# A weight's low word scaled and multiplied in one VectorE instruction, and two buffers for each conversion instead of three

## The chip, the cores and the metric

The kernel runs on one core of a Trainium2 chip. The metric is device time in microseconds; the kernel before took a median of 1023.06 us over 3 runs (1022.12 to 1026.41).

## What is computed

An attention layer feeds a mixing layer. Only the shapes and the arithmetic matter here; the weights `w_ch1` and `w_ch2` are 64-bit floats, all else is 32-bit.

```python
# attention: batch 4, 8 heads, 1152 keys, head size 64; queries pooled in pairs to 576
q_pool = q.reshape(B, H, S // 2, 2, D).mean(axis=3)
scores = np.matmul(q_pool, k.transpose(0, 1, 3, 2)) / np.sqrt(D)
attn = softmax(scores)                       # max subtracted, 1e-9 added to the sum
x = np.matmul(attn, v)                       # -> (B, 576, 512)
# mixing: real part of a 2-D FFT, layer norm, a feed-forward pair 512 -> 2048 -> 512
X = np.fft.fft(np.fft.fft(x, axis=1), axis=2)
u = x + np.real(X)
un = (u - u.mean(-1)) / np.sqrt(var(u) + 1e-6)
ch = np.maximum(un @ w_ch1, 0.0) @ w_ch2
return u + ch
```

## The kernel before

Attention runs over 16 pairs of heads, five units of 128 query columns to a pair. A unit has score matmuls (L220) whose negated, running-minimum copy VectorE takes out of PSUM (L222), an exponential on ScalarE (L234), transposes (L247) that ScalarE or VectorE copies out as `pt` (L250), and the product with `v` (L263, `o`). The queries and keys of the next heads are made meanwhile: GpSimd adds the two halves of `qr` (L186) and forms the low part of `ks` (L189), ScalarE casts `qh` (L194), GpSimd forms `ql` (L197).

Behind each batch of attention come its Fourier matmuls (`dft`: L501, L509), its norm (`norm`: L541 to L600) and its feed-forward (`ffn`): 32 blocks of weights for a batch, `w1` and `w2` in turns of four. A block is 12 matmuls of 128x512 at L689 to L691 (three products of high and low parts, four times). A block of `w1` ends in a ReLU on ScalarE (L708) and its low part `g` on VectorE (L709). These are fills between attention units.

The weights come as 64-bit floats. `convert` turns each of the 32 blocks into a high and a low 32-bit part once, while attention runs, and stores the result in DRAM, from where `wload` (L681) loads it for each batch. One conversion reads `wraw` from DRAM (L620, three buffers), takes the absolute value of the high word on ScalarE (L629), clamps, shifts, merges the sign and masks it on VectorE (L631, L633, L639, L642), scales the low word on ScalarE (`rest`, L635), casts the high part on ScalarE (L646), and then does three operations on GpSimd in two halves each (L649): `rest` times the power of two in `wa`, `wb` minus the high part, and the sum of the two. L655 stores it. `wa`, `rest` and `wb` are three tiles out of one ring of four (tag `cv`).

The order of all this is not left to a scheduler. The program keeps a clock of its own, `now`, which advances by what each step of attention yields; `after(wait, fn)` puts a step at a later point of that clock, and `convert` is a generator whose yields are such waits. So each engine's queue is a fixed list in order, and a yield that is changed moves instructions in it. `inside` lets one conversion at a time between its first ScalarE step and its last GpSimd step. `going` is non-empty once the first feed-forward has begun.

The ring `x` has five buffers for attention's results, each of which holds half a batch; where a sixth is wanted, `drain` stops attention and emits feed-forward blocks alone, each as soon as the plan has the conversion of the block two ahead in `wsc`. The first drain stands at about 430 to 470 us of the trace, beside the norm of batch 1; the last conversions are emitted within it. SyncE's queue issues nearly all DMAs, in order: raw weights (L620), stores (L655), loads (L681), and the heads' inputs (L126, L127).

## Time and profile before

| what | us |
|---|---|
| median of 3 runs | 1023.06 |
| the profiled execution | 1021.06 |
| its span, first to last instruction | 1019.3 |
| TensorE matmul busy | 968.8 |
| VectorE busy | 602.5 |
| ScalarE busy | 529.1 |
| GpSimd busy | 396.0 |

TensorE's busy time is modelled and overlaps from one matmul to the next, so a busy stretch isn't one at its peak. The conversions run from 80 us to 477 us; in that part of the span VectorE, ScalarE and GpSimd have most of their work. The profiled execution lies 2.0 us under the median.

### The profile page before, as it was taken

Reading aid. Unit: us, or ns where it says so; the run is one execution under the profiler, and the core shown is the slowest. Engines: PE = TensorE matmul, PEld = TensorE weight load, DVE = VectorE, ACT = ScalarE, POOL = GpSimd, SP = SyncE. Lnnn points to the kernel's source line nnn. Section 1 sums busy time; section 2 is a strip of 40 time slices with the busy share of each in tenths; the row PEclk is TensorE's granted clock in tenths of the full one; section 3 lists DMA queues with packets and bytes.
Section 4 is the critical chain, followed back from the end, with each engine's and each line's share of the span. In section 5 each row is a group of like instructions: output and inputs, shape, how many; then the busy total and the mean of one; then the engine's idle time right before and its main releaser. Section 6 shows DMA issues by size and latency. Waiting matters only on the chain.

```text
span 1019.3 us, 19742 instructions
## 1 busy us (share of the span) xinstructions
PE 968.8 (95%) x7392; PEld 841.5 (83%) x7392; DVE 602.5 (59%) x1526; ACT 529.1 (52%) x1033; POOL 396.0 (39%) x577
## 2 busy tenths in 40 slices
PE   6999988999999999978999999999999999899998
PEld 5898877777788887867888888788888878799998
DVE  5557787888756798866544465745644274422222
ACT  5777877758755575565644454535744221301100
POOL 3555678766666786874523232222400000000000
PEclk9999999999899999999999999999999999999999
DMA  6645458645385877566565453345432445733434
GB/s 181 176 142 183 130 189 255 191 139 167 119 255 208 280 242 235 182 235 197 175 194 164 135 184 120 90 150 161 130 116 83 145 137 165 219 131 128 128 124 124
DMA packets 62515, 170.91 MB, mean 168 GB/s; under 512 B 16770, under 2 KB 20242, under 8 KB 62420
## 3 DMA queue, kind: packets, MB, share of 16 engines
q1 hardware_dynamic: 58100, 151.96, 47.4%
q0 software_dynamic: 4320, 17.70, 5.5%
q8 instruction: 58, 0.95, 0.4%
q14 instruction: 37, 0.30, 0.1%
HBM read 146.88 MB, written 22.75 MB: 166 GB/s over the span
## 4 chain that ended last, share of the span: by engine, by line
PE 51%; DVE 3%; DMA 2%; ACT 1%; issue 1%; POOL 1%; SPq 0%; DVEq 0%; ACTq 0%
PE f L689 7%; PE f L691 6%; PE f L690 6%; PE o L263 6%; PE s L220 6%; PE t L247 5%; PE t L689 5%; PE t L691 5%; PE t L690 5%; DMA w<-w 1%; DVE sp L222 1%; DMA qr<-in_q 1%; PE f L509 1%; PE t L509 1%; ACT pt L250 0%
## 5 line engine op out<-in xcount | busy, mean ns | idle before, releaser
L222 DVE TENSOR_SCALAR_CACHE_REDUCE sp<-s,bia 128x384 f32<-128x384 f32 x288 | 177.5, 616 | 89.6 <-PE s L220 67.5
L220 PE MATMUL s<-ks,qh 128*128 128x384 f32 x480 | 185.1, 386 | 17.3 <-ACT qh L164 6.3
L234 ACT ACTIVATE sp<-sp,bia 128x1152 f32<-128x1152 f32 x144 | 180.2, 1255 | 5.7 <-DVE sp L222 5.4
L250 ACT COPY pt<-t 128x512 f32<-128x512 f32 (+2 forms) x243 | 124.7, 527 | 98.7 <-PE t L247 95.5
L263 PE MATMUL o<-pt,vs 128*64 128x128 f32 (+1 forms) x2880 | 168.1, 271 | 1.1 <-DVE pt L250 0.9
L263 PEld LDWEIGHTS o<-pt,vs 128*64 128x64 f32 x2880 | 148.9, 140 | 23.4 <-issue 20.1
L220 PE MATMUL s<-ks,ql 128*128 128x384 f32 x480 | 164.1, 342 | 0.9 <-POOL ql L197 0.9
L247 PE MATMUL t<-ident,sp 128*128 128x128 f32 x1045 | 151.7, 277 | 3.0 <-DVE sp L222 2.0
L247 PEld LDWEIGHTS t<-ident,sp 128*128 128x128 f32 x1045 | 121.0, 141 | 25.5 <-issue 7.0
L189 POOL TENSOR_TENSOR ks<-kr,ks 64x288 fp32r<-64x288 f32 x120 | 101.9, 880 | 37.3 <-issue 15.9
L220 PEld LDWEIGHTS s<-ks,qh 128*128 128x128 f32 x480 | 92.2, 192 | 28.1 <-ACT pt L250 10.1
L220 PEld LDWEIGHTS s<-ks,ql 128*128 128x128 f32 x480 | 92.6, 193 | 2.1 <-POOL ql L197 1.2
L709 DVE SCALAR_TENSOR_TENSOR g<-f,g 128x512 fp32r<-128x512 f32 (+1 forms) x49 | 32.5, 663 | 99.4 <-ACT g L708 99.4
L708 ACT ACTIVATE g<-f 128x512 fp32r<-128x512 f32 (+1 forms) x49 | 28.2, 576 | 120.0 <-PE f L691 120.0
L222 DVE TENSOR_SCALAR_CACHE_REDUCE sp<-s 128x384 f32<-128x384 f32 x144 | 78.7, 547 | 9.6 <-PE s L220 8.3
L197 POOL TENSOR_TENSOR ql<-qr,qh 128x288 fp32r<-128x288 f32 (+2 forms) x75 | 54.2, 747 | 75.6 <-ACT qh L194 74.6
L689 PE MATMUL f<-unh,w 128*128 128x512 f32 (+1 forms) x196 | 77.4, 395 | 6.3 <-DMA w<-w 5.8
L649 POOL TENSOR_TENSOR rest<-rest,wa 128x256 f32<-128x256 f32 x64 | 48.8, 781 | 88.9 <-DVE wa L642 69.9
L186 POOL TENSOR_TENSOR qr<-qr 128x288 f32<-128x288 f32 x60 | 48.1, 820 | 78.5 <-DMA qr<-in_q 78.5
L689 PE MATMUL f<-g,w 128*128 128x512 f32 (+1 forms) x192 | 76.0, 396 | 2.3 <-DMA w<-w 1.1
L691 PE MATMUL f<-unl,w 128*128 128x512 f32 (+1 forms) x196 | 75.1, 383 | 0.0
L690 PE MATMUL f<-unh,w 128*128 128x512 f32 (+1 forms) x196 | 74.8, 381 | 0.0
(146 smaller groups left out, 1749.8 us busy)
## 6 DMA issues: line engine op xcount, KB each, us to landing
w<-w SPq DMA_DIRECT2D x128, 512.0 KB, 3.6
qr<-in_q SPq DMA_DIRECT2D x30, 576.0 KB, 4.3
ks<-in_k POOLq DMA_DIRECT2D x30, 576.0 KB, 6.2
wraw<-in_w SPq DMA_DIRECT2D x32, 512.0 KB, 3.9
w<-wraw SPq DMA_DIRECT2D x32, 512.0 KB, 3.0
vs<-in_v SPq DMA_DIRECT2D x32, 288.0 KB, 7.0
kr<-in_k SPq DMA_DIRECT2D x30, 288.0 KB, 5.4
out<-x SPq DMA_DIRECT2D x12, 256.0 KB
```

The lines of the kernel that those rows point to most:

```text
L189: nc.gpsimd.tensor_tensor(ks[D:, c], kr[D:, c], ks[D:, c].bitcast(F32), op=ALU.subtract)
L197: nc.gpsimd.tensor_tensor(ql[:, z], qr[:, 0, x:y], qh[:, z].bitcast(F32), op=ALU.subtract)
L220: nc.tensor.matmul(ps, lhsT=l, rhs=k, start=i == 0, stop=i == len(ops) - 1)
L222: nc.vector.tensor_scalar(sp[n, j][:, c], ps, -0.0625, bt[:, pc - 1:pc] if pc else None, op0=ALU.mult, op1=ALU.min, accum_out=bt[:, pc:pc ...
L234: last_exp[0] = nc.scalar.activation(t, t, AF.Exp, bias=bia.pop((n, j))[:, 2:3], scale=-1.0, accum_out=den[pr][:, col:col + 1]).ins
L247: nc.tensor.transpose(ps[:, i * P:i * P + P], sp[k][:, c * P:(c + 1) * P], ident)
L250: (nc.vector.tensor_copy if eng == "v" else nc.scalar.copy)(pt[:, :o], ps[:, :o])
L263: nc.tensor.matmul(po[y * D:y * D + D, :w], lhsT=qkv[2 * pr + y][3][:, c, :], rhs=pt[:, o:o + w], start=c == 0, stop=c == NKC - 1)
L649: nc.gpsimd.tensor_tensor(o[:, c], x[:, c], y[:, c], op=op)
L689: nc.tensor.matmul(ps, lhsT=ah, rhs=bh, start=first, stop=False)
L690: nc.tensor.matmul(ps, lhsT=al, rhs=bh, start=False, stop=False)
L691: nc.tensor.matmul(ps, lhsT=ah, rhs=bl, start=False, stop=last)
```

## The change

The multiplication of the low word by 2^-52 (ScalarE, L635) and by the power of two in `wa` (GpSimd, two halves of L649) become one `scalar_tensor_tensor` on VectorE, L640 of the changed kernel, which reads the low words as 32-bit unsigned integers and writes over `wa`. The tile `rest` is gone, so a conversion takes two of the ring's four buffers. The yields change with it: the raw load is given 7000 instead of 6500 on the plan's clock once the feed-forward is going, there is one step more on VectorE before the cast, and the waits behind the cast are 2000 and 2600 instead of 3000 and 3000.

```diff
-        yield 6500 if going else 7000
+        yield 7000 if going else 7000
...
-        a = cvp.tile([P, 512], F32, tag="cv", name="wa", bufs=4)
-        ai = a.bitcast(I32)
+        a, t = (cvp.tile([P, 512], F32, tag="cv", name=x, bufs=4) for x in ("wa", "wb"))
+        ai, ti = a.bitcast(I32), t.bitcast(I32)
+        step = 700 if going else 1000
...
-        rest = cvp.tile([P, 512], F32, tag="cv", name="rest", bufs=4)
-        nc.scalar.activation(rest, low.bitcast(U32), AF.Copy, scale=2.0 ** -52)
...
-        nc.vector.tensor_scalar(ai, b, -0x800000, None, op0=ALU.bitwise_and)
-        yield 700 if going else 1000
+        nc.vector.tensor_scalar(ai, ti, -0x800000, None, op0=ALU.bitwise_and)
+        yield step
+        nc.vector.scalar_tensor_tensor(a, low.bitcast(U32), 2.0 ** -52, a, op0=ALU.mult, op1=ALU.mult)
+        yield step
...
-        for o, x, y, op in ((rest, rest, a, ALU.mult), (t, t, hi.bitcast(F32), ALU.subtract), (lo.bitcast(F32R), t, rest, ALU.add)):
+        for o, x, y, op in ((t, t, hi.bitcast(F32), ALU.subtract), (lo.bitcast(F32R), t, a, ALU.add)):
...
         if not going:
-            yield 3000
+            yield 2000
         inside.pop()
-        yield 3000 if going else 1500
+        yield 2600 if going else 1500
```

Lines behind the change stand two lower in the changed kernel: L649 becomes L647, L655 L653, L681 L679, L709 L707.

**GpSimd, the preparation of a pair's first head about 155 us into the trace.** `wb`, `wraw`, `rest`, `wa` are the conversion's tiles, `qr`, `ks`, `ql` the head's. Before:

```order
L649 TENSOR_TENSOR rest<-rest,wa 128x256 x2
L649 TENSOR_TENSOR wb<-wb,wraw 128x256 x2
L649 TENSOR_TENSOR wraw<-wb,rest 128x256 x2
L126 DMA ks<-in_k 128x1152
L137 MEMSET qh 128x64
L138 MEMSET ql 128x64
L186 TENSOR_TENSOR qr<-qr 128x288 x2
L189 TENSOR_TENSOR ks<-kr,ks 64x288 x4
L197 TENSOR_TENSOR ql<-qr,qh 128x288 x2
```

Now:

```order
L647 TENSOR_TENSOR wb<-wb,wraw 128x256 x2
L647 TENSOR_TENSOR wraw<-wb,wa 128x256 x2
L126 DMA ks<-in_k 128x1152
L137 MEMSET qh 128x64
L138 MEMSET ql 128x64
L186 TENSOR_TENSOR qr<-qr 128x288 x2
L189 TENSOR_TENSOR ks<-kr,ks 64x288 x4
L647 TENSOR_TENSOR wb<-wb,wraw 128x256 x2
L647 TENSOR_TENSOR wraw<-wb,wa 128x256 x2
L197 TENSOR_TENSOR ql<-qr,qh 128x288 x2
```

A conversion is four half operations instead of six, and the next conversion has slid in ahead of the head's `ql`.

**VectorE, two conversions in the first drain, with what each instruction waits for.** `g` is the ReLU's low part of a feed-forward block. Before:

```order
L639 SCALAR_TENSOR_TENSOR wb<-wraw,wa 128x512 [waits DMAHW7_49,DVE_49,Pool_49]
L642 TENSOR_SCALAR wa<-wb 128x512 [waits DVE_49]
L709 SCALAR_TENSOR_TENSOR g<-f,g 128x512 [waits Activation_49]
L631 TENSOR_SCALAR wa<-wa 128x512 [waits Activation_49]
L633 TENSOR_SCALAR wa<-wa 128x512 [waits DVE_49]
L639 SCALAR_TENSOR_TENSOR wb<-wraw,wa 128x512 [waits DMAHW2_49,DVE_49,Pool_49]
L709 SCALAR_TENSOR_TENSOR g<-f,g 128x512 [waits Activation_49]
```

Now:

```order
L636 SCALAR_TENSOR_TENSOR wb<-wraw,wa 128x512 [waits DMAHW1_49,DVE_49]
L707 SCALAR_TENSOR_TENSOR g<-f,g 128x512 [waits Activation_49]
L638 TENSOR_SCALAR wa<-wb 128x512 [waits DVE_49]
L640 SCALAR_TENSOR_TENSOR wa<-wraw,wa 128x512 [waits DVE_49]
L632 TENSOR_SCALAR wa<-wa 128x512 [waits Activation_49]
L634 TENSOR_SCALAR wa<-wa 128x512 [waits DVE_49]
L636 SCALAR_TENSOR_TENSOR wb<-wraw,wa 128x512 [waits DMAHW4_49,DVE_49]
L707 SCALAR_TENSOR_TENSOR g<-f,g 128x512 [waits Activation_49]
L638 TENSOR_SCALAR wa<-wb 128x512 [waits DVE_49]
```

The instruction that writes `wb` no longer waits for GpSimd; the `g` of a block now stands inside each conversion, ahead of its last two VectorE steps.

**SyncE, around the beginning of the first drain.** `w_10` to `w_15` are converted blocks of `w1` and then, from `w_12` on a second time, of `w2`; L655 (now L653) stores one, L681 (now L679) loads one for its feed-forward block. Before:

```order
L681 DMA w_5620<-w_10_5199 128x1024
L620 DMA wraw<-in_w 128x1024
L681 DMA w_5709<-w_11_5279 128x1024
L655 DMA w_14_5728<-wraw 128x1024
L681 DMA w_5760<-w_12_5387 128x1024
L681 DMA w_5783<-w_13_5561 128x1024
L681 DMA w_5807<-w_14_5728 128x1024
L620 DMA wraw<-in_w 128x1024
L655 DMA w_15_5830<-wraw 128x1024
L681 DMA w_5832<-w_15_5830 128x1024
L620 DMA wraw<-in_w 128x1024
L655 DMA w_12_5892<-wraw 128x1024
```

Now:

```order
L620 DMA wraw<-in_w 128x1024
L679 DMA w_5553<-w_10_5344 128x1024
L679 DMA w_5620<-w_11_5499 128x1024
L620 DMA wraw<-in_w 128x1024
L653 DMA w_12_5644<-wraw 128x1024
L679 DMA w_5647<-w_12_5644 128x1024
L620 DMA wraw<-in_w 128x1024
L653 DMA w_13_5699<-wraw 128x1024
L679 DMA w_5701<-w_13_5699 128x1024
L620 DMA wraw<-in_w 128x1024
L653 DMA w_14_5732<-wraw 128x1024
L679 DMA w_5734<-w_14_5732 128x1024
```

Before, blocks 12 to 14 are stored ahead of the loads of 12 to 14, and from block 15 on each load follows its own store; now this begins at block 12.

## Rows read from the trace of the kernel before

**Rows 1.** The page: the span, then busy us, share of the span and instructions by engine.

```profile
span 1019.3 us, 19742 instructions
...
PE 968.8 (95%) x7392; PEld 841.5 (83%) x7392; DVE 602.5 (59%) x1526; ACT 529.1 (52%) x1033; POOL 396.0 (39%) x577
```

**Rows 2.** Windows: busy us (instructions) of each engine, PE clock, DMA share, GB/s, by stretch.

```profile
125.00:175.00 50.00, 44.20 (x418) 37.96 (x414) 37.14 (x96) 37.24 (x75) 38.97 (x58) 0.97 0.66 202
175.00:250.00 75.00, 68.33 (x610) 55.30 (x612) 66.47 (x170) 54.68 (x108) 55.38 (x76) 0.99 0.53 165
375.00:425.00 50.00, 47.26 (x367) 38.35 (x364) 44.06 (x108) 31.12 (x65) 38.11 (x49) 1.00 0.53 174
425.00:480.00 55.00, 45.39 (x269) 37.16 (x268) 36.53 (x69) 30.24 (x54) 36.04 (x50) 0.94 0.71 237
```

**Rows 3.** Groups by form, 85 to 480 us: count, busy us, mean ns; idle before, its releasers.

```profile
L639 DVE SCALAR_TENSOR_TENSOR wb<-wraw,wa 128x512 int32<-128x512 int32 x32 | 26.8, 838 | 5.1 <-POOL wraw L649 4.7
...
L635 ACT ACTIVATE rest<-wraw 128x512 f32<-128x512 uint32 x32 | 21.8, 680 | 0.8 <-POOL rest L649 0.8
...
L633 DVE TENSOR_SCALAR wa<-wa 128x512 int32<-128x512 int32 x32 | 17.0, 530 | 0.3
...
L646 ACT CAST wraw<-wb 128x512 fp32r<-128x512 f32 x32 | 19.8, 620 | 9.1 <-issue 5.2 <-DVE wb L639 3.7
...
L649 POOL TENSOR_TENSOR rest<-rest,wa 128x256 f32<-128x256 f32 x64 | 48.8, 781 | 88.9 <-DVE wa L642 69.9 <-ACT wraw L646 9.0 <-ACT sp L234 4.7
```

**Rows 4.** Waits, whole span: who waited for whom, us in total, times, longest us.

```profile
ACT qh L194 <- POOL qr L186: 14.1, 8, 3.4
...
PE s L220 <- ACT pt L250: 5.8, 9, 1.8
...
PE f L247 <- ACT pt L250: 4.9, 9, 1.6
```

**Rows 5.** Timeline: start us, us, instruction, [idle before <-releaser]; POOL, ACT, PE, 133 to 159 us.

```profile
151.23 1.42 POOL L649 TENSOR_TENSOR rest<-rest,wa 128x256 f32<-128x256 f32 x2 [3.25 <-ACT wraw L646]
...
155.54 1.55 POOL L186 TENSOR_TENSOR qr<-qr 128x288 f32<-128x288 f32 x2
...
134.68 0.76 ACT L194 CAST qh<-qr 128x512 fp32r<-128x512 f32 x2 [2.18 <-POOL qr L186]
...
157.12 0.67 ACT L194 CAST qh<-qr 128x576 fp32r<-128x576 f32 x1 [3.37 <-POOL qr L186]
...
135.99 0.66 PE L247 MATMUL f<-ident,sp 128*128 128x128 f32 x4 [1.63 <-ACT pt L250]
...
158.33 0.45 PE L220 MATMUL s<-ks,qh 128*128 128x384 f32 x1 [1.14 <-ACT pt L250]
```

**Rows 6.** Timeline of ACT, DVE and PE in the first drain, 433 to 470 us.

```profile
433.16 0.66 ACT L629 ACTIVATE wa<-wraw 128x512 f32<-128x512 f32 x1 [5.33 <-DMA wraw<-in_w]
...
454.37 0.69 DVE L639 SCALAR_TENSOR_TENSOR wb<-wraw,wa 128x512 int32<-128x512 int32 x1 [2.67 <-POOL wraw L649]
...
460.24 0.69 DVE L639 SCALAR_TENSOR_TENSOR wb<-wraw,wa 128x512 int32<-128x512 int32 x1 [1.98 <-POOL wraw L649]
...
454.22 0.77 PE L689 MATMUL f<-unh,w 128*128 128x512 f32 x1 [3.09 <-DMA w<-w]
...
461.59 0.75 PE L581 MATMUL f<-dg,onesm 96*128 96x288 f32 x2 [2.58 <-DVE g L709]
...
463.30 0.47 PE L689 MATMUL f<-g,w 128*128 128x512 f32 x1 [0.95 <-PE f L581]
...
470.01 0.39 PE L690 MATMUL f<-g,w 128*128 128x512 f32 x1
470.23 0.39 PE L691 MATMUL f<-g,w 128*128 128x512 f32 x1
```

**Rows 7.** The page's DMA issues: KB each, median us from issue to landing.

```profile
wraw<-in_w SPq DMA_DIRECT2D x32, 512.0 KB, 3.9
...
w<-wraw SPq DMA_DIRECT2D x32, 512.0 KB, 3.0
```

More of the change, by code (lines that the diff above doesn't have):

```diff
@@ L631, in convert @@
         nc.vector.tensor_scalar(a, a, WORD_MIN, WORD_MAX, op0=ALU.max, op1=ALU.min)
-        yield 700 if going else 1000
+        yield step
         nc.vector.tensor_scalar(ai, ai, 3, 0x3FFFFFF8, op0=ALU.logical_shift_left, op1=ALU.bitwise_and)
-        rest = cvp.tile([P, 512], F32, tag="cv", name="rest", bufs=4)
-        nc.scalar.activation(rest, low.bitcast(U32), AF.Copy, scale=2.0 ** -52)
-        yield 700 if going else 1000
-        t = cvp.tile([P, 512], F32, tag="cv", name="wb", bufs=4)
-        b = t.bitcast(I32)
-        nc.vector.scalar_tensor_tensor(b, high, -0x40000000, ai, op0=ALU.bitwise_and, op1=ALU.bitwise_or)
-        yield 700 if going else 1000
-        nc.vector.tensor_scalar(ai, b, -0x800000, None, op0=ALU.bitwise_and)
-        yield 700 if going else 1000
+        yield step
+        nc.vector.scalar_tensor_tensor(ti, high, -0x40000000, ai, op0=ALU.bitwise_and, op1=ALU.bitwise_or)
+        yield step
+        nc.vector.tensor_scalar(ai, ti, -0x800000, None, op0=ALU.bitwise_and)
+        yield step
+        nc.vector.scalar_tensor_tensor(a, low.bitcast(U32), 2.0 ** -52, a, op0=ALU.mult, op1=ALU.mult)
+        yield step
         h = w.rearrange("p c x -> p (c x)").rearrange("p (x c) -> p x c", x=2)
```

## The prediction

> **What bounds the kernel now.** I read the page first: TensorE's matmuls are busy for 968.8 of 1019.3 us, the next engine for 602.5 [rows 1]. So only TensorE's gaps, some 50 us, and stretches at a lower clock can be won, and work taken from ScalarE or GpSimd pays only where TensorE waits for it. The table by stretch tells where that is: 5.8 of 50 us are missing between 125 and 175 us, 6.7 of 75 up to 250, 2.7 of 50 from 375 to 425, and 9.6 of 55 after that, at a mean clock of 0.97, 0.99, 1.00 and 0.94 [rows 2]. All of these lie in the time of the conversions. VectorE is the fullest helper there, with 66.47 of 75 us and 44.06 of 50; ScalarE has 37.24 of the first 50, GpSimd 38.97. The waits then tell by whom: TensorE waits for the copies `pt` of ScalarE and VectorE (5.8 and 4.9 us), and behind some of those ScalarE itself has waited for GpSimd, 14.1 us in 8 waits at the cast `qh` [rows 4].
>
> The timeline shows such a chain twice. At 151.23 us GpSimd begins a conversion, after 3.25 us of waiting for ScalarE's cast; the queries' addition behind it in the queue comes at 155.54; ScalarE's `qh` has stood 3.37 us for it by 157.12, and TensorE 1.14 us for a `pt` behind that. Around 135 us it is 2.18 and 1.63 us [rows 5]. The first drain has another: VectorE stands 2.67 and 1.98 us before it may write `wb`, because the ring of four buffers gives it one that GpSimd still reads; the `g` of a feed-forward block is behind it in VectorE's queue, and TensorE waits 2.58 us for that `g` and 0.95 more. A weight load there ends 3.09 us late, after a raw load for which ScalarE had waited 5.33 us [rows 6].
>
> **The change, part by part.** *Work that goes.* ScalarE loses 32 instructions of 0.68 us, 21.8 us; GpSimd loses 64 half operations of 0.781 us, 48.8 us [rows 3]. Nearly all of it lies beside other work. GpSimd was idle for 88.9 us ahead of the first pair of these operations, 2.8 us for each conversion [rows 3]: where it waits, the time is set by the one who hands over. That is now ScalarE's cast, which stands one VectorE step later in the plan. Of a conversion's GpSimd end, 2 x 0.78 = 1.56 us are saved and up to 0.84 given back (the new step, below): 0.7 us sooner at the least where nothing else moves, 1.56 where GpSimd was behind.
>
> What that gives TensorE goes by the 14.1 us [rows 4]. In the two chains shown 5.55 us of ScalarE's waiting became 2.77 us of TensorE's [rows 5], one half, so those waits are worth about 7 us. Eight waits shorter by 0.7 to 1.56 us give 8 x 0.7 / 2 = 2.8 to 8 x 1.56 / 2 = 6.2 us. Against it stands the order: the next conversion now slips in ahead of a head's `ql`, which TensorE needs for its scores; one such place at 4 x 0.78 = 3.1 us could take back all of the lower figure. I take 4 us gained, and keep 0 and 6.2. ScalarE's 0.68 us apiece are worth at most part of the 10.7 us that TensorE waits for `pt` [rows 4]; one instruction less in some 12 us, with ScalarE three quarters full, is 1 us, between 0 and 2.
>
> *Work that comes.* The new instruction isn't in the trace. Its nearest row is L639, same engine, same kind, one input in the same strided words, same size: 0.838 us on average, 26.8 us for 32 [rows 3]. Its other bound is a single-input step of the same size, 0.53 us (17.0 us for 32) [rows 3]. I take 0.84, since two inputs are what both share. The Trainium skill (SBUF — State Buffer, "Who interferes with whom") says that a VectorE instruction with two SBUF inputs contends with GpSimd instructions that read SBUF; by that rule an instruction could stand for a whole GpSimd half operation, 1.6 us apiece and 16 us for the ten below, and the time would be 1031 if all of it reached TensorE. The trace of before can't tell that from another cause: it shows a mean of 0.838 us for L639 beside a busy GpSimd [rows 3].
>
> Where VectorE is fullest (175 to 250 and 375 to 425 us), 125 us hold about 10 conversions at 390 us for 32. They bring 10 x 0.84 = 8.4 us onto VectorE, which has 14.5 us free there [rows 2]. So between 0 and 8.4 us reach TensorE. 2 us is my value: VectorE rises to some 95%, not to the end, and GpSimd's lighter load lets it go a little faster. The change hands work of ScalarE to the engine that is fullest here. The Trainium skill (Perfetto Trace Analysis, "Optimizing Scalar/DVE Operations") advises the reverse where VectorE is saturated; the trace has it at 89% at most in these stretches [rows 2], so it doesn't decide the matter, and the slower rival below is what the rule would make of it.
>
> *Two buffers instead of three.* The wait of `wb` for GpSimd is gone from the order. In the drain that frees 2.58 + 0.95 = 3.5 us of TensorE [rows 6].
>
> *What is moved.* A conversion now has one step more on the plan's clock and a longer lead for its load, so conversions come later against the feed-forward. In SyncE's order each load follows its own store from block 12 on, where it was from block 15 on: three more blocks of the drain go at the conversions' pace. A block is 12 matmuls some 0.22 us apart [rows 6], 2.7 us. A conversion's pace with three raw buffers is a third of its round: raw load 3.9, store 3.0 [rows 7], and between them absolute value (as L635) 0.68, three single-input steps at 0.53, two double ones at 0.84, cast 0.62 and four GpSimd halves at 0.78 [rows 3], 7.7 us, in all 14.6 / 3 = 4.9 us. Three blocks cost 3 x (4.9 - 2.7) = 6.6 us if nothing runs ahead and 0 if attention hides it. I take 2.5, because conversions still run during the attention ahead of the drain. The late raw load (3.09 us of TensorE) has a fair chance to go with the longer lead, 1 us of gain. With the 3.5 us above the drain comes to -2 us; its ends are -3.5 - 3.1 = -6.6 and +6.6.
>
> *Clock.* The granted clock was 0.97 from 125 to 175 us, 1.5 us of those 50, and 0.94 after 425, 3.3 us of 55 [rows 2]; TensorE had stood before. Less standing there gives back 1 us, at most 3, and more standing takes as much.
>
> *Sum.* -4 (GpSimd's chain) -1 (ScalarE) +2 (VectorE) -2 (drain) -1 (clock) = -6 us. The profiled execution took 1021.06 us, of which 1.8 lie outside its span, and would take 1015; the median is 2.0 us above it, so 1017.
>
> **Rivals.** *VectorE becomes the bound (slower).* The new instruction stands in VectorE's queue ahead of the score copies L222 and, in the drain, with the last mask step between one block's `g` and the cast, so that conversion and block wait for each other. Price: all 8.4 us in place of 2 in the full stretches, and 4 instead of -2 in the drain, 1017 + 6.4 + 6 = 1029 us. For it speaks VectorE's 89% [rows 2]; against it that the rest of the span has room. It decides if VectorE is busy for over 96% of a stretch of 25 us or more in which TensorE idles.
>
> *The work leaves idle engines (no change).* GpSimd waited anyway [rows 3], the cast comes later, and heads wait as before; the drain's saved ring wait is paid back by the three later blocks. Then the sum is 0 to -2 us: 1021 to 1023 us.
>
> *The drain is freed (larger gain).* Its 6.6 us of idle time [rows 6] and its 3.3 us of slow clock go, and the waits for GpSimd go by the upper figure: -9.9 - 6.2 + 2 = -14 us, 1009. For it speaks that the buffers' wait was the pace from one conversion to the next, 460.24 - 454.37 = 5.9 us, against the 4.9 worked out; against it, that three more blocks now need that pace.
>
> **How the numbers follow.** The forecast, 1017 us with 1012 to 1021 around it, gets 0.42; the slower rival 0.23; no change 0.2; the larger gain 0.15. Half a per cent, about what a measurement of this kernel can tell, is 5.1 us, or 1018. Under it lie the larger gain and two thirds of the forecast, 0.43; over 1028 us the slower rival and what the drain's upper end adds to it, 0.23; between them 0.34. The range from 1008 to 1029 leaves out a third of the slower rival and a little at the other end, which is 2 in 10 with what none of the cases has.
>
> **What would show it.** Right: ScalarE's wait for `qr` falls from 14.1 us to about 8; no VectorE wait for GpSimd at `wb`; the new instruction takes 0.7 to 0.9 us; TensorE's idle time between 125 and 175 us falls by 2 us or more. Wrong: VectorE over 96% busy with TensorE waiting for L222; TensorE standing 1 to 2 us before each of the blocks 12 to 15 of the drain, for its weight load, with the drain longer by more than 4 us; a new wait of scores for `ql`.

## The result and the profile after

The changed kernel took a median of 1033.43 us (1031.19 to 1037.49, 4 runs) where the kernel before took 1022.59 (1021.11 to 1026.41, 4 runs) beside it: a ratio of 1.0121, 95% interval 1.0085 to 1.0157. It is 1.2% slower; the forecast was 1017, and 1029 the upper end of its range. The profiled execution took 1031.19 us.

The head of the page of the changed kernel answers to [rows 1]:

```profile
span 1029.3 us, 19688 instructions
...
PE 970.1 (94%) x7392; PEld 841.3 (82%) x7392; DVE 617.5 (60%) x1558; ACT 511.5 (50%) x1001; POOL 355.5 (35%) x513
```

TensorE has the same 7392 matmuls. The work went where the diff says: VectorE +15.0 us, ScalarE -17.6, GpSimd -40.5. The stretches of [rows 2], same columns:

```profile
125.00:175.00 50.00, 46.61 (x482) 41.38 (x479) 44.46 (x112) 39.58 (x80) 36.50 (x50) 1.00 0.69 219
175.00:250.00 75.00, 69.95 (x615) 57.61 (x613) 64.26 (x175) 52.40 (x107) 45.30 (x61) 0.98 0.56 173
375.00:425.00 50.00, 44.33 (x342) 34.85 (x339) 42.33 (x103) 26.38 (x54) 27.77 (x39) 1.00 0.63 196
425.00:480.00 55.00, 38.42 (x138) 29.04 (x137) 40.70 (x67) 21.36 (x39) 27.39 (x33) 0.81 0.57 200
```

In the first two TensorE is busier than before, 46.61 for 44.20 us and 69.95 for 68.33; in the third it is less busy, 44.33 for 47.26. In the last it is busy for 38.42 us in place of 45.39, at a clock of 0.81 in place of 0.94. The groups by form from 85 to 480 us, as [rows 3]:

```profile
L647 POOL TENSOR_TENSOR wb<-wb,wraw 128x256 f32<-128x256 f32 x62 | 46.6, 771 | 122.9 <-ACT wraw L644 105.0 <-issue 14.4 <-DVE x L521 3.1
...
L636 DVE SCALAR_TENSOR_TENSOR wb<-wraw,wa 128x512 int32<-128x512 int32 x32 | 24.7, 772 | 0.4
...
L640 DVE SCALAR_TENSOR_TENSOR wa<-wraw,wa 128x512 f32<-128x512 uint32 x31 | 22.1, 713 | 0.2
...
L644 ACT CAST wraw<-wb 128x512 fp32r<-128x512 f32 x31 | 19.2, 619 | 24.4 <-DVE wa L640 10.7 <-issue 10.0 <-ACT sp L234 2.8
```

The new instruction takes 0.713 us on average. `wb` no longer waits for GpSimd (0.4 us idle, none of it for GpSimd). But ScalarE's cast, which stood 9.1 us, now stands 24.4. The waits, as [rows 4]:

```profile
PE f L687 <- DMA w<-w: 10.6, 5, 3.9
...
PE f L561 <- DVE sq L556: 5.4, 3, 2.5
PE s L220 <- DVE sp L222: 5.3, 7, 1.8
...
ACT qh L194 <- POOL qr L186: 3.0, 5, 1.7
```

ScalarE's wait for `qr` fell from 14.1 to 3.0 us; the longest of TensorE's own waits is the one for weight loads, 10.6 us (6.8 before).

**Where the time went.** I number the units of attention from 0 by their `o` matmuls (L263) in TensorE's timeline, and compare the times at which the same unit begins, with 2.72 us for each feed-forward block that one kernel has done more. Unit 34 stands ahead of the first feed-forward; the first drain lies between units 46 and 47.

| begin of unit | before | changed | difference, blocks allowed for |
|---|---|---|---|
| 15 | 116.6 | 117.1 | +0.5 |
| 34 | 275.8 | 266.1 | -9.6 |
| 46 | 420.0 (20 blocks) | 413.0 (19 blocks) | -4.3 |
| 47 | 470.6 (30) | 481.6 (30) | +11.0 |
| 78 | 788.6 (70 blocks) | 794.9 (69) | +8.9 |

So the change first gained 9.6 us, gave 5 back by unit 46, and lost 15 in the first drain. One window over just that drain, for the changed kernel:

```profile
412.94:481.55 68.61, 51.19 (x223) 39.27 (x223) 50.91 (x91) 27.77 (x49) 35.26 (x45) 0.85 0.62 210
```

and for the kernel before:

```profile
419.96:470.60 50.64, 41.34 (x211) 33.10 (x210) 35.88 (x68) 26.56 (x49) 35.47 (x47) 0.93 0.66 232
```

TensorE idles 17.4 instead of 9.3 us, and at a mean clock of 0.85 instead of 0.93 it loses up to 10.3 instead of 3.5 us (all of it, if the lower clock fell on work alone): 8.1 + 6.8 = 14.9 us of the 15.3 by which the drain is longer, a block allowed for. The changed kernel's timeline there, SyncE's queue, TensorE and ScalarE's first step of a conversion (start, duration, instruction, [idle before]):

```profile
450.02 0.32 SPq L653 DMA_DIRECT2D w<-wraw  x1
453.73 0.32 SPq L679 DMA_DIRECT2D w<-w  x1
454.10 0.42 SPq L620 DMA_DIRECT2D wraw<-in_w  x1
...
460.13 0.32 SPq L679 DMA_DIRECT2D w<-w  x1
...
468.42 0.32 SPq L653 DMA_DIRECT2D w<-wraw  x1
474.88 0.32 SPq L679 DMA_DIRECT2D w<-w  x1
...
449.73 0.77 PE L687 MATMUL f<-unh,w 128*128 128x512 f32 x1 [3.86 <-DMA w<-w]
457.44 0.47 PE L687 MATMUL f<-unh,w 128*128 128x512 f32 x1 [2.25 <-DMA w<-w]
463.86 0.77 PE L687 MATMUL f<-unh,w 128*128 128x512 f32 x1 [3.44 <-DVE wa L640]
...
458.89 0.67 ACT L630 ACTIVATE wa<-wraw 128x512 f32<-128x512 f32 x1 [0.59 <-DMA wraw<-in_w]
466.17 0.70 ACT L630 ACTIVATE wa<-wraw 128x512 f32<-128x512 f32 x1 [1.71 <-DMA wraw<-in_w]
473.61 0.68 ACT L630 ACTIVATE wa<-wraw 128x512 f32<-128x512 f32 x1
```

Three blocks in a row begin after 2.25 to 3.86 us of standing. (The view puts the third down to VectorE's `wa`, which no block reads; its weight load had gone out at 460.13, 3.7 us before it began.) Conversions come 7.3 to 7.4 us apart, and three weight loads take 474.88 - 453.73 = 21.15 us, 7.05 each. The store at 450.02 is followed by its block's load 3.7 us later, the one at 468.42 by its own 6.5 us later, and the next raw load stands behind the load (454.10). At 24 conversions begun by unit 46, eight are left for the drain; the kernel before had begun 27 and had five left.

### The profile page after: what moved, and what is told of

The parts are those of the page before. It is cut to its first block, busy times and chain, and to the rows that moved or that the text cites. A ratio compares the mean times of both kernels' runs of the same rounds, so it can differ in the third digit from the quotient of the medians.

```text
span 1029.3 us, 19688 instructions
## 1 busy us (share of the span) xinstructions
PE 970.1 (94%) x7392; PEld 841.3 (82%) x7392; DVE 617.5 (60%) x1558; ACT 511.5 (50%) x1001; POOL 355.5 (35%) x513
## 4 chain that ended last, share of the span: by engine, by line
PE 74%; DVE 12%; ACT 4%; issue 4%; DMA 3%; POOL 1%; SPq 0%; DVEq 0%; ACTq 0%; POOLq 0%
PE o L263 12%; PE s L220 12%; PE t L247 8%; PE f L687 8%; PE f L689 7%; PE f L688 7%; PE t L687 5%; PE t L689 5%; PE t L688 5%; DVE sp L222 4%; PE f L247 3%; PE f L509 2%; ACT pt L250 1%; DMA w<-w 1%; ACT sp L234 1%
## 5 line engine op out<-in xcount | busy, mean ns | idle before, releaser
L263 PE MATMUL o<-pt,vs 128*64 128x128 f32 (+1 forms) x2880 | 165.4, 267 | 4.8 <-DVE pt L250 4.6
L263 PEld LDWEIGHTS o<-pt,vs 128*64 128x64 f32 x2880 | 145.8, 138 | 27.6 <-issue 19.7
L707 DVE SCALAR_TENSOR_TENSOR g<-f,g 128x512 fp32r<-128x512 f32 (+1 forms) x49 | 32.5, 663 | 103.2 <-ACT g L706 103.2
L647 POOL TENSOR_TENSOR wb<-wb,wraw 128x256 f32<-128x256 f32 x64 | 48.0, 769 | 127.0 <-ACT wraw L644 109.1
L687 PE MATMUL f<-unh,w 128*128 128x512 f32 (+1 forms) x196 | 79.1, 404 | 10.6 <-DMA w<-w 6.7
L197 POOL TENSOR_TENSOR ql<-qr,qh 128x288 fp32r<-128x288 f32 (+2 forms) x75 | 56.8, 782 | 72.7 <-ACT qh L194 71.9
L186 POOL TENSOR_TENSOR qr<-qr 128x288 f32<-128x288 f32 x60 | 49.8, 850 | 77.4 <-DMA qr<-in_q 77.4
L688 PE MATMUL f<-unh,w 128*128 128x512 f32 (+1 forms) x196 | 76.2, 389 | 0.0
```

What stands on the lines that cost most here:

```text
L186: nc.gpsimd.tensor_tensor(qr[:, 0, c], qr[:, 0, c], qr[:, 1, c], op=ALU.add)
L197: nc.gpsimd.tensor_tensor(ql[:, z], qr[:, 0, x:y], qh[:, z].bitcast(F32), op=ALU.subtract)
L263: nc.tensor.matmul(po[y * D:y * D + D, :w], lhsT=qkv[2 * pr + y][3][:, c, :], rhs=pt[:, o:o + w], start=c == 0, stop=c == NKC - 1)
L687: nc.tensor.matmul(ps, lhsT=ah, rhs=bh, start=first, stop=False)
L688: nc.tensor.matmul(ps, lhsT=al, rhs=bh, start=False, stop=False)
```

## The experiments

All times are medians beside runs of the kernel before on the same chip; a ratio is to those. "Lead" is the difference to before at unit 34 (negative is ahead), "begun" the conversions begun by unit 46, "drain" the time from unit 46 to 47, which holds 10 blocks, 11 where marked. "Start" is the plan's time of the first conversion. "Old yields" are those of before; "new until" means the new ones until the first feed-forward and the old ones after it.

| kernel | instruction | yields | start | us | ratio, interval | lead | begun | drain |
|---|---|---|---|---|---|---|---|---|
| before | old | old | 60000 | - | 1 | 0 | 27 | 50.6 |
| changed | new | new | 60000 | 1033.4 | 1.0121, 1.0085 to 1.0157 | -9.6 | 24 | 68.6 (11) |
| e1 | new | old | 60000 | 1020.5 | 0.9983, 0.9957 to 1.0009 | -1.5 | 27 | 49.6 |
| e2 | old | new | 60000 | 1030.6 | 1.008, 1.005 to 1.011 | -8.4 | 24 | 67.3 (11) |
| e3, ring of 3 | new | old | 60000 | 1023.2 | 1.0004, 0.9977 to 1.0031 | +0.6 | 27 | 50.6 |
| e4 | new | new | 36000 | 1027.6 | 1.0041, 1.0013 to 1.007 | -8.7 | 26 | 58.2 |
| e5 | new | new until | 60000 | 1034.4 | 1.0129, 1.0104 to 1.0154 | -9.7 | 26 | 61.5 |
| e6 | new | new from | 60000 | 1040.7 | 1.0193, 1.0168 to 1.0218 | -2.2 | 25 | 59.9 |
| e8 | new | new until | 50000 | 1011.1 | 0.99, 0.988 to 0.9921 | -9.2 | 27 | 50.5 |
| e9 | new | old | 36000 | 1021.7 | 1.0007, 0.9991 to 1.0022 | +5.1 | 29 | 47.0 |
| e10, own tile | new | old | 60000 | 1022.7 | 1.0014, 0.9988 to 1.0039 | -1.8 | 27 | 49.8 |
| e11, raw by GpSimd | new | new | 60000 | 1044.4 | 1.0216, 1.0174 to 1.0257 | -2.3 | 24 | 69.2 (11) |
| e12 | old | new until | 50000 | 1009.4 | 0.987, 0.9822 to 0.9917 | -13.8 | 27 | 51.0 |
| e13 | new | new until | 45000 | 1012.4 | 0.9908, 0.9875 to 0.9941 | -2.2 | 28 | 46.3 |
| e14 | new | old | 50000 | 1025.1 | 1.0042, 1.0027 to 1.0057 | +1.4 | 27 | 50.8 |
| e14 | new | old | 45000 | 1014.4 | 0.9927, 0.9897 to 0.9957 | -3.2 | 28 | 46.3 |
| e15 | old | old | 50000 | 1021.7 | 1.0004, 0.9986 to 1.0021 | -4.5 | 27 | 51.2 |
| e16 | new | new until | 55000 | 1018.2 | 0.9969, 0.9951 to 0.9987 | -5.4 | 27 | 50.2 |
| e17, grouped | new | new | 60000 | 1037.4 | 1.0185, 1.0148 to 1.0222 | -10.6 | 24 | 68.4 (11) |
| e18, grouped | new | new until | 50000 | 1013.9 | 0.9939, 0.9917 to 0.9961 | -9.6 | 27 | 50.8 |

Kernels that are alike up to unit 34 (e1 and e6; the changed one, e5 and e17; e8 and e18) lie within 1.0 us of each other there; so a lead is good to about that. Leads and drains are read from one execution each; that of e17 took 5.0 us less than its kernel's median, those of e5 and e16 3.4 and 3.2 less, that of e14 at 50000 3.3 more.

**First: is it the instruction or the yields?** e1 is the changed kernel with the yields of before:

```diff
-        yield 7000 if going else 7000
+        yield 6500 if going else 7000
...
         nc.vector.tensor_scalar(ai, ti, -0x800000, None, op0=ALU.bitwise_and)
-        yield step
...
-            yield 2000
+            yield 3000
         inside.pop()
-        yield 2600 if going else 1500
+        yield 3000 if going else 1500
```

> The changed kernel's instructions and its two buffers, on the plan of the kernel before: the new VectorE instruction is issued in the same step as the mask ahead of it, and the yields are those of before, so that every conversion stands where it stood. Theory L (lateness: the yields made the conversions late, and the first drain pays 15 us for it; the instruction itself costs nothing that can be measured): 1008 to 1018 us, the drain no longer than before's (TensorE's last unit before it to the first behind it, 50.6 us in the trace of before, 68.6 in the changed one). Theory V (VectorE: the new instruction in its queue sets the conversions' pace and holds up the blocks): 1028 to 1034 us with the drain still over 60 us.

e2 is the reverse, the old instructions with the new yields and an empty step where the new instruction would be:

> The kernel before with the yields of the changed one and one empty step where the new instruction would be issued: ScalarE and GpSimd still do the low word in three buffers, but the conversions come as late as in the changed kernel. Theory L: 1030 to 1042 us, and the drain 66 us or more, since the ring of three buffers holds each conversion up besides. Theory V: 1018 to 1026 us, drain 50 to 56 us. The gain before the drain tells who made it: TensorE ahead of before by 6 us or more at 275 us would be the order's work, by under 3 us the instruction's.

Theory V would have e1 slower than before, and it isn't; it isn't faster either, 2.5 us above the range of theory L; e2 has the whole pattern of the changed kernel, the lead (-8.4) and the drain (67.3 us). So the yields made both the gain and the loss, and the instruction, at this start, neither. e1 also shows what became of the forecast's main gain. The cast's row of e1, from 85 to 275 us:

```profile
L643 ACT CAST wraw<-wb 128x512 fp32r<-128x512 f32 x13 | 8.0, 619 | 18.7 <-DVE wa L639 13.9 <-issue 3.8 <-ACT pt L250 1.0
...
L194 ACT CAST qh<-qr 128x576 fp32r<-128x576 f32 (+2 forms) x15 | 7.2, 514 | 2.5 <-POOL qr L186 2.5
```

In the kernel before, the same two rows had 1.3 and 9.5 us of idle time. ScalarE waits less for GpSimd and more for VectorE: the cast writes its result over raw words that the new instruction still has to read, so it now waits for two VectorE instructions more. From unit 9 to 34 TensorE idled 21.1 us in e1 and 16.6 before, and lost 0 us instead of some 7 (summed over stretches of 20 us) to the clock.

**The ring.** e3 is e1 with three buffers in place of four, which brings the wait for GpSimd back:

```diff
-        a, t = (cvp.tile([P, 512], F32, tag="cv", name=x, bufs=4) for x in ("wa", "wb"))
+        a, t = (cvp.tile([P, 512], F32, tag="cv", name=x, bufs=3) for x in ("wa", "wb"))
```

> The first experiment (new instruction, old plan) with a ring of three small buffers instead of four, so that the writer of wb has to wait again for GpSimd's last sum of the conversion before, as in the kernel before. If that wait is worth the 3.5 us of the prediction: 3 to 4 us above the first experiment, with VectorE waits for GpSimd of some 5 us in all at wb and TensorE waiting in the drain for a block's low part. If conversions in the drain are paced by the DMA round and not by the ring: within 2 us of it.

The drain is 50.6 against 49.6 us. The medians are 1023.2 and 1020.5, the means of ten executions each, taken side by side, 1022.7 and 1020.6. So the ring's wait was worth 1 us in the drain and about 2 in all, between the two expectations.

**An earlier first conversion.** e4 is the changed kernel with `cdue = 36000.0` in place of `60000.0`:

> The changed kernel with one number changed: the plan's first conversion is issued at 36 instead of 60 us, so some two conversions more are done by the drain. Theory L: the drain is shorter by 10 us or more, 1018 to 1025 us, the gain ahead of the drain kept. Theory V: VectorE's share per conversion is the same and the drain's pace too, so under 5 us are won, 1028 us or more.

Two conversions more are begun by unit 46, the drain is 10.4 us shorter (7.7 beside the block that it holds less), and 6 us of the loss are won back. The time lies between the ranges of the two theories, nearer to V's; but the drain is shorter as L said, so lateness is a cause, if not of the whole loss.

**Which yields?** e5 takes the new yields back from the first feed-forward on, e6 until it:

```diff
@@ e5, against the changed kernel @@
-        yield 7000 if going else 7000
+        yield 6500 if going else 7000
...
-        yield step
+        if not going:
+            yield step
...
-        yield 2600 if going else 1500
+        yield 3000 if going else 1500
@@ e6, against the changed kernel @@
-        yield step
+        if going:
+            yield step
...
-            yield 2000
+            yield 3000
```

> The changed kernel whose yields are those of before from the first feed-forward on; until then the new yields stay. Theory S (two separate places): the changed yields ahead of the feed-forward made TensorE's lead of 8 to 10 us at the 34th unit, and those behind it made the loss of 15 us in the first drain. Then the lead stays (7 us or more at unit 34), the drain takes 50 to 58 us instead of 68.6, and the time is 1010 to 1018 us. Theory D (a debt): the lead is conversions put off, which the drain has to make up whichever yields did it; then lead and loss go together, and the time is 1022 to 1031 us.

> The counterpart: the changed kernel with the yields of before until the first feed-forward, and the new ones from there on. Theory S: no lead at unit 34 (under 3 us), and a drain 8 to 15 us longer than before: 1027 to 1037 us. Theory D: no lead and no debt, 1018 to 1024 us.

e8 is e5 with `cdue = 50000.0`, and e9 is e1 with `cdue = 36000.0`:

> As the kernel with the new yields until the feed-forward alone, with the first conversion given out at 50000 of the plan's clock instead of 60000, so that one conversion more is done ahead of the drain. If a conversion left for the drain costs TensorE some 5 us there (theory S), the drain is as short as that of before, 50 us, or shorter, with a lead of 7 us or more ahead of it: 1008 to 1015 us. Theory D: 1019 to 1024 us.

> The new instruction and two buffers with the yields of before, and the first conversion at 36000 of the plan's clock instead of 60000: two or three conversions more are done ahead of the drain. If each conversion left for the drain costs 4 to 5 us there and none ahead of it, the drain falls from 50 us to about 40 and the time to 1010 to 1014 us. If a conversion costs the attention ahead as much, 1018 to 1023 us.

The lead goes with the yields ahead of the feed-forward, as theory S said (e5 -9.7, e6 -2.2). But S had the time of e5 wrong by 16 us: I had taken its drain for that of before, and it begins with one conversion fewer. By itself e5 speaks for theory D, with lead and loss together, though 3 us above D's range. D falls by the other two: e6 has no lead and loses all the same, and e8 has the lead and the short drain, and at 1011.1 us it beats both kernels. What goes with the drain's length is the number begun by unit 46: 27 before, 26 in e5, 25 in e6, 24 with both changes. e5 and e8 differ in the start of the conversions alone; their windows over the drain, e5:

```profile
414.27:475.75 61.48, 46.18 (x209) 36.74 (x208) 42.55 (x75) 24.16 (x45) 30.86 (x40) 0.83 0.56 200
```

and e8:

```profile
412.94:463.46 50.52, 43.17 (x209) 34.46 (x208) 40.01 (x73) 22.99 (x43) 27.71 (x36) 0.86 0.67 236
```

With the same 209 matmuls, one conversion more that is left over costs e5 11 us, 15.3 of TensorE's idle time against 7.4. Over all the kernels with 27 begun the drain is 49.6 to 51.2 us, with 28 or 29 it is 46.3 to 47.0, with 25 or 26 it is 58.2 to 61.5, with 24 it is 67.3 to 69.2 with a block more, about 65.5 without. From 27 down to 24 a conversion left over costs 5 us on average ((65.5 - 50.5) / 3), but not evenly: e5 with 26 has a longer drain than e6 with 25. From 27 to 28 another 4 us are won, from 28 to 29 nothing, and e9, with 29, had paid 5 us ahead of it.

The drain isn't the whole of the loss. In e6, whose time is 4 us above the range of S, the stretch from unit 34 to 46 has lost 11.5 us before the drain begins; e6 first, then before:

```profile
273.56:429.36 155.80, 144.79 (x1081) 120.99 (x1080) 116.93 (x274) 82.68 (x163) 81.69 (x110) 0.98 0.64 205
...
275.75:420.01 144.26, 141.47 (x1080) 118.59 (x1079) 110.59 (x263) 90.76 (x178) 102.77 (x141) 1.00 0.70 229
```

The other kernels take 145.2 to 151.3 us for it, a block allowed for. No run takes this stretch apart.

**Does the cast's wait eat the gain?** e10 is e1 with a tile of its own for the cast:

```diff
-        nc.scalar.copy(hi.bitcast(F32R), t)
-        for o, x, y, op in ((t, t, hi.bitcast(F32), ALU.subtract), (lo.bitcast(F32R), t, a, ALU.add)):
+        own = cvp.tile([P, 512], F32, tag="cv", name="own", bufs=4)
+        nc.scalar.copy(own.bitcast(F32R), t)
+        for o, x, y, op in ((t, t, own, ALU.subtract), (lo.bitcast(F32R), t, a, ALU.add)):
...
-        nc.sync.dma_start(d, h.bitcast(F32))
+        nc.sync.dma_start(d[:, 0, :], own)
+        nc.sync.dma_start(d[:, 1, :], lo.bitcast(F32))
```

> The new instruction with the yields of before, but ScalarE's cast writes to a tile of its own (a third buffer of the ring of four) instead of over the raw words, which the new instruction still reads; the store becomes two of half the size. In the kernel with the new instruction and the yields of before, ScalarE stood 18.7 us at that cast from 85 to 275 us, 13.9 of them for VectorE, where the kernel before stood 1.3. Theory W (the cast's wait for the new instruction is what ate the gain): the wait falls under 7 us and TensorE is 5 to 9 us ahead at the 34th unit: 1011 to 1017 us. Theory E (VectorE's fuller queue ate it, whatever the cast waits for): TensorE is within 3 us of before there and the time 1018 to 1025 us.

The cast's row of e10, from 85 to 275 us:

```profile
L644 ACT CAST own<-wb 128x512 fp32r<-128x512 f32 x13 | 8.1, 624 | 1.6 <-DVE wb L636 1.6
```

The wait is gone, 1.6 us for 18.7, and TensorE is 1.8 us ahead at unit 34 where e1 was 1.5. So theory W falls: in this stretch neither of ScalarE's two waits was what TensorE paid for. What rose in e1 was TensorE's waiting for VectorE; its groups from 116 to 275 us, with their idle time:

```profile
L220 PE MATMUL s<-ks,qh 128*128 128x384 f32 x116 | 44.8, 386 | 5.6 <-DVE sp L222 3.2 <-ACT pt L250 2.1 <-issue 0.2
L263 PE MATMUL o<-pt,vs 128*64 128x128 f32 (+1 forms) x708 | 42.9, 267 | 3.9 <-DVE pt L250 3.6 <-ACT pt L250 0.2
...
L247 PE MATMUL t<-ident,sp 128*128 128x128 f32 x256 | 37.4, 278 | 4.7 <-DVE sp L222 2.8 <-ACT sp L234 1.8
```

The kernel before has 2.3, 0.7 and 1.2 us in place of 3.2, 3.6 and 2.8: 5.4 us more.

**What sets the pace in the drain?** e11 issues the raw loads from GpSimd's queue; e17 issues VectorE's last three steps of a conversion together, so that no block's `g` stands between them, with every other step of the plan where it was:

```diff
@@ e11, against the changed kernel @@
-        nc.sync.dma_start(w, src[f].bitcast(I32).rearrange("p (c x) -> p c x", x=2))
+        nc.gpsimd.dma_start(w, src[f].bitcast(I32).rearrange("p (c x) -> p c x", x=2))
@@ e17, against the changed kernel @@
-        yield step
+        if not going:
+            yield step
...
-        yield step
+        if not going:
+            yield step
...
+        if going:
+            yield step
+            yield step
```

> The changed kernel with the raw loads issued from GpSimd's queue instead of SyncE's, where each stands behind a weight load that waits for a store to land. Theory Q (this queue sets the pace of the conversions in the first drain): the raw loads go out 2 us or more sooner, the conversions come every 5 to 5.5 us instead of 6.7, and the drain falls from 68.6 to 60 us or less; 1022 to 1028 us. Theory V (VectorE's instructions behind the blocks' g set it, or the store and its load themselves): the drain stays over 65 us and the time at 1030 to 1036 us.

> The changed kernel in which, from the first feed-forward on, VectorE's mask and the new instruction are issued in the same step as the merge ahead of them, with the yields behind; everything else stands at the same time of the plan. So a block's g no longer stands between the merge and the mask. Theory G (in the first drain the conversions go round through the blocks: load, block, ReLU, g, mask, new instruction, cast, GpSimd, store, and three of them share one turn of 21.2 us): the cast waits 1.5 to 2.5 us less for each conversion, the pace falls from 7.05 us to 5 to 6.3, and the drain from 68.6 to 60 to 65 us; 1024 to 1030 us. Theory H (ScalarE's queue, in which the cast stands behind the block's ReLU anyway, or the store and load themselves, hold the pace): over 66 us, 1031 to 1036 us.

In e11 a raw load goes out well ahead of the weight load behind which it stood (GpSimd's queue, SyncE's, and ScalarE's first step of a conversion):

```profile
459.58 0.57 POOL L620 DMA_DIRECT2D wraw<-in_w  x1
...
463.08 0.32 SPq L679 DMA_DIRECT2D w<-w  x1
...
457.83 0.67 ACT L630 ACTIVATE wa<-wraw 128x512 f32<-128x512 f32 x1 [1.24 <-DMA wraw<-in_w]
```

The drain stays at 69.2 us, so theory Q falls. That doesn't take the raw load out of the round: it now stands behind GpSimd's half operations, and ScalarE still waits 1.24 us for it at 457.83. (Of the 13.4 us by which the span of e11 is longer than the changed kernel's, 7.3 are the lead that it has lost, -2.3 for -9.6; the rest was not followed up.) In e17 VectorE does its steps together, with no `g` in between (VectorE, ScalarE, TensorE):

```profile
451.06 1.09 DVE L636 SCALAR_TENSOR_TENSOR wb<-wraw,wa 128x512 int32<-128x512 int32 x1
452.19 0.83 DVE L639 TENSOR_SCALAR wa<-wb 128x512 int32<-128x512 int32 x1
453.06 0.69 DVE L642 SCALAR_TENSOR_TENSOR wa<-wraw,wa 128x512 f32<-128x512 uint32 x1
...
464.62 0.60 ACT L711 ACTIVATE g<-f 128x512 fp32r<-128x512 f32 x1 [3.62 <-PE f L694]
465.11 0.61 ACT L649 CAST wraw<-wb 128x512 fp32r<-128x512 f32 x1
...
451.95 0.77 PE L692 MATMUL f<-unh,w 128*128 128x512 f32 x1 [3.37 <-DMA w<-w]
459.12 0.77 PE L692 MATMUL f<-unh,w 128*128 128x512 f32 x1 [2.78 <-DMA w<-w]
```

The drain is 68.4 us, so theory G's forecast falls, and the blocks still stand for their loads. TensorE did idle 1.6 us less in this drain than in the changed kernel's (15.8 for 17.4), but at a clock of 0.80 for 0.85 it lost 3.4 more. At 464.62 us the cast has another obstacle: ScalarE stands 3.62 us at the ReLU for TensorE, whose block had itself begun 2.78 us late at 459.12, and the cast comes right behind. e18, the same grouping in e8, gains nothing either (50.8 us of drain for 50.5, and a ratio of 0.9939 for 0.99):

> The same grouping in the fastest kernel with the new instruction (new yields until the feed-forward, first conversion at 50000; 1011 us), whose drain took 50.5 us with 7.4 us of TensorE's idle time. Theory G: 2 to 5 us less, 1006 to 1009 us. Theory H: 1009 to 1013 us.

What is left of the loop is store, load, block, ReLU, cast, GpSimd, store; that it sets the pace is read from the timeline and not shown. Moving the raw loads to another queue or taking `g` out from between VectorE's steps didn't shorten it, and no run took out another link. The time from store to load isn't it by itself: it grows to 6.5 us in the changed kernel and stays at 2.6 to 3.0 in e2, whose drain is as long. The clock is in the loop too: the block at 449.73 runs at the lower level and takes 2.4 us longer, and no run parts that from the standing.

**Is the lead the yields', or the start's?** Six kernels: e12 is the kernel before with the step of 1000 ahead of the cast, 2000 in place of 3000 behind it and `cdue = 50000.0`; e13 and e16 are e8 at 45000 and 55000; e14 is e1 at 50000 and 45000; e15 is the kernel before at 50000.

```diff
@@ e12, against the kernel before @@
         nc.vector.tensor_scalar(ai, b, -0x800000, None, op0=ALU.bitwise_and)
         yield 700 if going else 1000
+        if not going:
+            yield 1000
...
-            yield 3000
+            yield 2000
...
-    cdue = 60000.0
+    cdue = 50000.0
```

> The kernel before with the new yields until the first feed-forward (a step of 1000 ahead of the cast, 2000 behind it in place of 3000) and the first conversion at 50000; ScalarE's and GpSimd's old instructions stay. It is the fastest kernel so far without the new instruction. Theory P (the plan alone makes the gain): 1009 to 1014 us, the same as with the new instruction. Theory I (the instruction earns its part once the cast no longer waits for it): 1015 to 1021 us.

> The fastest kernel so far (new yields until the feed-forward, first conversion at 50000) with the first conversion at 45000, so that one conversion fewer is left for the drain. If a conversion less in the drain still gains there, 1005 to 1010 us; if the drain is already bound by its blocks and the norm, or the conversion costs the attention as much, 1010 to 1016 us.

> The new instruction and two buffers with the yields of before and the first conversion at 50000, as the fastest kernel with the new instruction has it; so it differs from that one in the step ahead of the cast alone. So far three kernels with the new yields were 8.7 to 9.7 us ahead of before at the 34th unit and one, started at 45000, only 2.2; those with the old yields stood at -1.5 and, started at 36000, at +5.1. Theory C (the step ahead of the cast makes the lead): under 4 us ahead at unit 34, 1015 to 1024 us. Theory F (where the conversions fall against the units of attention makes it, and the start moves them): 7 us or more ahead, 1008 to 1014 us.

> The same with the first conversion at 45000, the start at which the new yields gave a lead of only 2.2 us. Theory C: about 7 us behind that kernel, so 3 to 6 us behind before at unit 34, and 1017 to 1025 us. Theory F: anything between 6 us behind and 10 ahead; within 2 us of the kernel with the new yields at this start would say that the step does nothing there.

> The kernel before with nothing changed but the first conversion at 50000 instead of 60000. Theory C: no lead at unit 34 (under 4 us), 1016 to 1024 us. Theory F: a lead of 7 us or more, 1008 to 1014 us. It also tells what the step alone is worth to the old instructions, against the kernel of 1009.4 us that differs from it in the step alone.

> The new yields until the feed-forward, with the first conversion at 55000. Its drain has the steps of the kernel started at 50000, so its time shows the lead: theory C expects 8 to 10 us of it and 1009 to 1013 us. Theory F expects a value that goes with neither neighbour: under 5 us of lead and 1014 to 1021 us would speak for it.

New against old yields at the same start and with the same instruction, the lead grows by 13.8 us (start 36000), 10.6 (50000) and 8.1 (60000), with the old instructions by 9.3 (50000) and 8.4 (60000), and at 45000 it doesn't (-2.2 against -3.2). So the yields make a lead in five pairs of six. Theory C as it was expected holds less well: e15 has a lead of 4.5 us where it allowed 4, e16 5.4 where it wanted 8, and e14 at 45000 is ahead by 3.2 where it was to be behind. The start moves the lead by several us besides (e16 lies between kernels with -9.2 and -9.7), and so does the queue of the raw loads (e11), so a part of theory F is true too. Why a cast that is 1000 later on the plan's clock does this was not taken apart further: TensorE's idle time from unit 9 to 34 is 11.5 to 14.6 us in the eight kernels with a lead of over 8 us, and 16.6 to 23.5 in all others. What this stretch's order does to each wait stays open.

The new instruction, at the same yields and start, changes unit 34 by -1.2 us (new yields, 60000), -1.5 (old, 60000), +4.6 (new, 50000) and +5.9 (old, 50000): a loss of 1.9 us on average. In the last of these pairs the whole times say so too, 1025.1 us (e14) and 1021.7 (e15) side by side, with intervals that don't meet. The kernel with the lowest median, e12 at 1009.4 us, hasn't got it; its interval overlaps that of e8, which has. The page of e12:

```profile
span 1008.0 us, 19738 instructions
...
PE 964.3 (96%) x7392; PEld 840.3 (83%) x7392; DVE 601.8 (60%) x1526; ACT 528.8 (52%) x1033; POOL 396.8 (39%) x577
```

## Why the prediction was wrong

*What held.* `wb` waits no more for GpSimd, the new instruction took 0.7 us, and `ql` brought no new wait. TensorE's idle time from 125 to 175 us fell by 2.4 us (5.8 to 3.4), but that sign came true by luck: the yields made it. With the instruction and the old yields (e1, first) it is 4.6, without the instruction and with the new ones (e2) 2.7:

```profile
125.00:175.00 50.00, 45.39 (x446) 39.03 (x448) 40.87 (x104) 39.97 (x79) 33.64 (x50) 1.00 0.70 222
...
125.00:175.00 50.00, 47.34 (x481) 42.00 (x478) 43.18 (x112) 41.51 (x84) 38.47 (x55) 1.00 0.68 219
```

*GpSimd's chain, -4 us, and ScalarE, -1.* The wait for `qr` fell as said, further than to the 8 us named (3.0). That half of it would reach TensorE was wrong: with the old yields (e1) it fell to 4.0 us over the span, and TensorE gained 1.5 us by unit 34, less than the clock alone gave back. The wait was followed by another: ScalarE's cast waits for VectorE, and TensorE waits for VectorE's copies. e10 then showed that ScalarE's waiting had little to do with TensorE's. The 5.8 and 4.9 us of TensorE's waits for `pt` were put down to ScalarE and VectorE; both rows name ScalarE's copies. In e1 they are 4.0 and 4.9, 1.8 us less where 1 was taken.

*VectorE, +2 us.* Its mechanism was right. In the two stretches of this term TensorE idled 1.8 us more in e1 than before (66.30 and 47.46 us busy for 68.33 and 47.26), about as taken; over the longer stretch from 116 to 275 us it waited 5.4 us more for VectorE. The new instruction took 0.713 us where 0.84 was taken: the mean of L639 holds one instruction of 3.8 us, and its median is 0.69 (ns, least, median, most):

```profile
L639 DVE SCALAR_TENSOR_TENSOR wb<-wraw,wa x32: 670/690/3799, 93.6 to 470.6; 128x512 int32<-128x512 int32 x32
```

The estimate from the rule of the Trainium skill (SBUF — State Buffer, "Who interferes with whom") was up to 1.6 us; the mean shows nothing of that size, and the longest took 1.04 us.

*The yields.* The text counted them only for what they delay. Ahead of the feed-forward they gained 8 to 10 us, more than all the terms of the sum together; no term had this.

*The drain, -2 us: here the forecast failed.* Its sign for the wrong case came true in kind and larger than named: TensorE stood 2.25 to 3.86 us before three of the blocks 12 to 15 (all but the first), and the drain was longer by 15 us where the upper end was 6.6. Three steps of that term were off. Three later blocks was right (27 less 24), but "conversions still run during the attention ahead" took 6.6 down to 2.5, which was wrong: as the drain opened, the conversions begun were five ahead of the blocks done (24 and 19), where they had been seven (27 and 20). The pace was worked out from a round of raw load, conversion and store, 4.9 us; it was 7.05, 3 x (7.05 - 2.7) = 13 us for the three blocks. That a block which waits for the conversion stands in the round too is how the timeline reads, and isn't shown. And the clock was given a gain of 1 us, at most 3 either way; it lost up to 6.8 us more in the drain, where TensorE stood more, a part of which is in the 13. The 3.5 us of the ring's wait were 1 in the drain (e3).

*The rivals.* The slower one had the right side, 1029 us, and its sign can be seen from 150 to 175 us (the changed kernel, then before): VectorE is busy for 24.14 of 25 us, 96.6%, and TensorE idles 3.4 us where it had idled 2.4.

```profile
150.00:175.00 25.00, 21.63 (x208) 18.79 (x208) 24.14 (x53) 19.00 (x39) 18.48 (x23) 1.00 0.65 210
...
150.00:175.00 25.00, 22.61 (x200) 19.00 (x198) 18.18 (x47) 18.99 (x38) 19.67 (x29) 0.93 0.84 249
```

But VectorE is as good as full there by the yields: it is busy for 21.26 us in e1, which has the instruction, and for 23.37 in e2, which hasn't. The rival's mechanism, the new instruction in VectorE's queue, isn't what made the kernel slow: e1 has it and isn't slower, e2 hasn't and is.

## What to carry to other kernels

Where an order is written out by a plan's clock, undo the yields and the instruction apart from each other before believing either: here the edit that was named gained nothing, and the waits around it made a gain of 9 and a loss of 15 us. Work that must be done by a certain point is best read as a count at that point (conversions begun when the drain opens): between e8 and e5 one fewer made the drain 11 us longer, though e6 with another fewer paid no more there. What the removal of a wait is worth on an engine off the critical path isn't known until the next wait behind it is.

## What the runs showed of the hardware

A lower granted clock (a mean between its two levels, 1.2 and 2.4 GHz) came with TensorE's standing, and cost nearly as much: in the drain 8.1 us more of idle time came with up to 6.8 us more lost at the lower level, the block at 449.73 us of the changed kernel then taking 0.43 us from matmul to matmul, 5.1 us for twelve, instead of 2.7. The loss doesn't follow the amount of standing, though: the drain of before idled 9.3 us and lost 3.5, that of e8 idled 7.4 and lost some 7, that of e17 idled 15.8 and lost 13.7. Ahead of unit 34 the same kind of loss came and went with small edits, 0 us in e1, some 3 to 4 in e3, some 7 before.

VectorE's steps were not equally long. In e17 the merge took 1.09 us at 451.06 and the single-input mask 0.83 at 452.19, while GpSimd's halves of the conversion before ran until 452.7; one conversion earlier, with GpSimd idle, the same two took 0.68 and 0.43:

```profile
446.51 0.68 DVE L636 SCALAR_TENSOR_TENSOR wb<-wraw,wa 128x512 int32<-128x512 int32 x1
447.23 0.43 DVE L639 TENSOR_SCALAR wa<-wb 128x512 int32<-128x512 int32 x1
```

Each gained about 0.4 us, half of a GpSimd half operation (0.8). It isn't so each time: of the 32 new instructions of the changed kernel 28 took 0.67 to 0.69 us and four 0.76 to 1.04, all four while GpSimd was busy. The Trainium skill (SBUF — State Buffer, "Who interferes with whom") lets an instruction that comes second wait until the first one ends; the trace doesn't speak against it, but in this kernel it puts the price at 0.4 us or less for the new instruction, not at the 1.6 of the prediction's estimate.
